# A conditioned transformer block on one core: query features scaled within FFN1, attention products at parts seven and ten of FFN2

## The chip, the cores and the metric

The kernel runs on one core of a Trainium2 chip. The metric is the device time of one execution in microseconds (us). Engines are named as in the profile: PE is TensorE (PEld its weight loads), DVE is VectorE, ACT is ScalarE, POOL is GpSimd, SP is SyncE, which here only issues DMAs. All times in the text are microseconds from the start of the profiled span unless said otherwise.

## The reference

A layer of 2048 rows of 576 with adaptive layer norm: linear attention with a softmax feature map in 32 heads of 18, then a dense ReLU network of width 4608. Cut to what matters:

```python
def _A_ref(x, wqkv, w_phi, wo):                  # per head, Dh = 18
    q, k, v = split(x @ wqkv)
    pq, pk = q @ w_phi, k @ w_phi
    phi_q = concat([softmax(pq), softmax(-pq)])
    phi_k = concat([softmax(pk), softmax(-pk)])
    kv, z = phi_k.T @ v, sum(phi_k, over rows)
    o = (phi_q @ kv) / (phi_q @ z + 1e-6)
    return o @ wo

sa, ca, ga, sb, cb, gb = split(silu(c) @ w_mod, 6)
x = x + ga * _A_ref(layernorm(x) * (1 + ca) + sa, ...)
h = layernorm(x) * (1 + cb) + sb
x = x + gb * (maximum(h @ w1, 0) @ w2)
```

## The kernel before

Rows are kept 128 to a tile, 16 tiles; a block is U = 2 tiles, so there are NQ = 8 blocks, 0 to 7. Everything up to the sum over keys (`kv`), and all of block 0's second half of the layer, runs in an order written out by hand, a string of steps. After it `block(n)` runs for n = 1 to 7, and the change lies in that function alone. Each engine executes its instructions in the order in which the code issues them, and waits where an operand or a buffer isn't ready; nothing is reordered.

`block(n)` does the dense network of block n, and between its matmuls two other jobs. The next block m = n + 1 gets its attention finished: output projection (`wo_rows`), residual, second layer norm, transposed into hT. The block after, n + 2, gets its query features made and its attention products taken.

**FFN1** (`ffn1_rows`, matmuls on line 827, ReLU on line 872). Nine pairs q of hidden tiles. Each is computed in two phases, "a" and "b", which use the two halves of the array's rows crosswise; the order on PE is a0, a1, b0, a2, b1, a3, b2 and so on to a8, b7, b8. Between a pair's phases stands a tiny POOL write, the token of line 831: phase b waits for it, and it waits for phase a. After b of pair q, ACT does the ReLU of q into H1. The products of a pair lie in one of three PSUM buffers (`mm_tile`), so phase a of pair q + 3 needs the ReLU of q. The dictionary `behind` says which other work is issued behind which phase: ("b", 5) is behind phase b of pair 5 and its ReLU.

**FFN2** (`ffn2_step`, line 910). For each of the two row tiles j and the two column halves (0 and 288) three parts of 12 matmuls, twelve parts in all. Part 0 takes one of the same three PSUM buffers, first that of FFN1's pair 6. Parts 0, 1 and 2 of each read the ReLUs of pairs 0 to 2, 3 to 5 and 6 to 8. After part 2 DVE scales the output (line 918), adds the residual (919), and after the second half SP sends it out (921).

**The features of block n + 2** (`softmax_parts`, in two tiles' E): `low` and `high` subtract the minimum and maximum (DVE, lines 464 to 479), `exps(j)` the exponential of tile j (ACT, 506), `sums(j)` their sums (DVE, 524), `recip` the reciprocal by Ln and Exp (ACT, 529 and 531), `scale` the scaling (DVE, 541, two instructions). `q_T` issues two DMA transposes on SP's queue (653), one for each tile, into ET. In traces E carries the name room.

**The attention products** `attention(m, j)`: `num` is 11 small matmuls (666) into the two aux PSUM buffers; `quotient` divides on DVE (674 to 681); `o_T` is a DMA transpose on SP (689). The aux buffers are also those of `wo_rows`.

**The next block's norm**: `late(j)` is the second phase of `wo_rows` (matmuls of line 827 too), the residual add on DVE (728) and the statistics on DVE (226, 227). `norm_out` is `rstd` on ACT (233, 234), the normalisation on DVE (238, two instructions), a copy (423), and two DMA transposes on SP into hT (425). `mods` scales hT in place on DVE (418, five instructions).

Before the change, the features of n + 2 are made in FFN1 up to the sums of tile 0. The sums of tile 1 come behind `norm_out` after FFN1; `recip`, `scale` and `q_T` come after FFN2's first three parts, behind their output on DVE. The products of tile 0 follow FFN2's seventh part, those of tile 1 the tenth. Block 1 differs in that it also takes the products of block 2, in FFN1. Block 6 has no features to make, block 7 no other work at all.

Of the kernel before, what the change touches and what calls it, by code (L numbers as in the profile page):

```python
# [21 lines left out]
NQ = NT // U  # L22
# [21 lines left out]
def kernel(  # L44
# [34 lines left out]
    def mm_tile(name):  # L79
        return mmp.tile([P, 2, 512], FP32, name=name, tag="mm")  # L80

    def aux_tile(name, dt=FP32):
        t = aux.tile([P, 512], FP32, name=name, tag="aux")
        return t if dt == FP32 else t.bitcast(BF16)
# [365 lines left out]
    HALVES = [(0, 288), (288, 288)]  # L450
# [148 lines left out]
    def q_soft(n):  # L599
        E = Eqs[n % 2]  # L600
        if n < 2:
            G.memset(E[:, :, :, DW:], 0.0)
        Es[n] = E
        b, u = n // 2, n % 2
        return softmax_parts(E[:, :, :, 0:DW], pq[b][:, u * U:(u + 1) * U], U, False)
# [42 lines left out]
    def q_T(n):  # L648
        E = Es[n]
        ET = work.tile([P, NG, U, P], BF16, name="ET", tag="ET", bufs=2)  # L650
        ETs[n] = ET
        for j in range(U):
            nc.sync.dma_start_transpose(out=ET[:, :, j, :], in_=E[:, j].rearrange("p g c -> p (g c)"))

    def num(n, j):

        ET = ETs[n]
        if n == 0:
            ps = mm_tile("ps_num")
            ps = (ps[:, 0], ps[:, 1])  # L660
        else:
            ps = (aux_tile("ps_num"), aux_tile("ps_nun"))
        onum[n, j] = ps
        for g in range(NG):
            o = (g % GB) * GV
            T_.matmul(ps[g // GB][:, o:o + gcols(g)], lhsT=ET[0:DW, g, j, :], rhs=KVZ[0:DW, g, 0:gcols(g)],  # L666
                      start=True, stop=True)
# [156 lines left out]
    def row_halves(key, phase, items):  # L824

        for k, (ps, l, r) in enumerate(items):
            i = T_.matmul(ps, lhsT=l, rhs=r, start=(phase == 0 and k < 2), stop=(phase == 1 and k >= len(items) - 2))  # L827
            if phase == 1 and k == 0:
                tc.add_manual_dep(i.ins, last[key].ins.name, AFTER, reason="same banks, other rows")
        if phase == 0:  # L830
            g = last[key] = G.memset(token[:], 0.0)  # L831
            tc.add_manual_dep(g.ins, i.ins.name, AFTER, reason="products of one half of the rows done")

    def f1_rows(n, q, phase):

        hT, w, items = hT2[n], U * P, []
        if phase == 0:
            f1_open(n, (q,))
        for hh in range(2):
            for ci in ((4, 0, 1, 2, 3) if phase == 0 else (0, 1, 2, 3)):  # L840
                for r in range(2):
                    s, e = slice(r * 64, r * 64 + 64), r ^ phase
                    l = w1["c"][s, 2 * q + hh, :] if ci == 4 else w1_at(2 * q + hh, e, ci, s)
                    items.append((f1[q][:, e, hh * w:hh * w + w], l, hT[s, ci, :]))
        row_halves(("f1", q), phase, items)

    def wo_rows(n, j, phase):

        if phase == 0:
            onum["wo", n, j] = [aux_tile("ps_wo") for _ in HALVES]  # L850
        items = []
        for ci in ((4, 0, 1, 2, 3) if phase == 0 else (0, 1, 2, 3)):
            for r in range(2):
                s, e = slice(r * 64, r * 64 + 64), r ^ phase
                items.append((onum["wo", n, j][e][:, 0:288], oTs[n, j][s, ci, :], wo_sb[s, ci, e * 288:e * 288 + 288]))
        row_halves(("wo", j), phase, items)

    def ffn1_rows(n, behind={}):

        for k in range(NI // 2 + 1):  # L860
            for p in (0, 1):
                q = k - p
                if k == 0 and p == 1 or q > NI // 2 - 1:
                    continue
                f1_rows(n, q, p)
                if p:
                    f1_relu(q)
                if ("ab"[p], q) in behind:
                    behind["ab"[p], q]()

    def f1_relu(q):
        A_.activation(out=p2t["H1"].rearrange("p (e j) n -> p e j n", e=2)[:, :, 2 * q:2 * q + 2],  # L872
                      in_=f1[q][:].rearrange("p e (h n) -> p e h n", h=2), func=ACT.Relu)
# [27 lines left out]
    def ffn2_step(n, j, cs, cn, part):  # L901

        if part == 0:
            f2[j, cs] = mm_tile("ps_y")
            if ("o", n, j) not in f2:
                f2["o", n, j], f2["sent"] = p2t["p2"].tile([P, D], BF16, name="outt", tag="outt", bufs=2), 0
        ps, o = f2[j, cs], f2["o", n, j]
        c = slice(cs, cs + cn)
        for k in [e * NI + part * 6 + i for e in range(2) for i in range(6)]:
            T_.matmul(ps[:, 0, 0:cn], lhsT=p2t["H1"][:, k, j * P:(j + 1) * P], rhs=p2t["w2"][:, k, c],  # L910
                      start=(k == 0), stop=(k == NJ - 1))
        if part == 2 and n > 0:
            ffn2_out(n, j, cs, cn)

    def ffn2_out(n, j, cs, cn):
        ps, o = f2[j, cs], f2["o", n, j]
        c = slice(cs, cs + cn)
        V.tensor_tensor(out=o[:, c], in0=ps[:, 0, 0:cn], in1=rows["gb"][:, c], op=ALU.mult)  # L918
        V.tensor_tensor(out=o[:, c], in0=o[:, c], in1=x_sb[:, n * U + j, c], op=ALU.add)
        if cs + cn == D or (n, j) == (NQ - 1, U - 1):  # L920
            nc.sync.dma_start(outv[:, n * U + j, f2["sent"]:cs + cn], o[:, f2["sent"]:cs + cn])
            f2["sent"] = cs + cn if cs + cn < D else 0

    def y(n, j, cols=HALVES):
        for cs, cn in cols:
            for part in range(3):
                ffn2_step(n, j, cs, cn, part)
# [74 lines left out]
    def block(n):  # L1002


        m = n + 1 if n + 1 < NQ else None
        if m is None:
            ffn1_rows(n)
            y(n, 0)

            y(n, 1, ((0, 288), (288, 192), (480, 96)))  # L1010
            return
        soft_ = q_soft(n + 2) if n + 2 < NQ else None
        xn, stats, rstd, norm = norm_stats(m * U, U)

        def do(name, *a):
            if soft_ is not None:
                getattr(soft_, name)(*a)

        def attention(m, j):
            num(m, j)  # L1020
            quotient(m, j)
            o_T(m, j)

        def late(j):
            wo_rows(m, j, 1)
            wo_out(m, j)
            stats(j)

        def norm_out():
            rstd()  # L1030
            norm()
            norm_dma(xn, U, new_hT2(m), 0)

        def mods():
            for ci in range(KC):
                modulate(V, hT2[m][:, ci, :], hT2[m][:, ci, :], mod[2], ci)

        def both(*fs):
            return lambda: [f() for f in fs]

        if n == 1:
            do("low")
            do("high")
            ffn1_rows(n, {("b", 0): lambda: attention(m, 0), ("b", 2): lambda: attention(m, 1), ("b", 3): lambda: do("exps", 0),
                          ("b", 4): both(lambda: wo_rows(m, 0, 0), lambda: do("exps", 1)), ("b", 5): both(lambda: late(0), lambda: do("sums", 0)),
                          ("a", 8): lambda: wo_rows(m, 1, 0), ("b", 7): lambda: late(1)})
        else:
            ffn1_rows(n, {("a", 0): both(lambda: do("low"), lambda: do("high")), ("b", 1): lambda: wo_rows(m, 0, 0),
                          ("b", 2): lambda: late(0), ("b", 3): lambda: do("exps", 0), ("b", 4): both(lambda: wo_rows(m, 1, 0), lambda: do("exps", 1)),
                          ("b", 5): both(lambda: late(1), lambda: do("sums", 0))})  # L1050
        norm_out()
        do("sums", 1)
        y(n, 0, HALVES[:1])
        do("recip", 0)
        do("scale", 0)
        if n + 2 < NQ:
            q_T(n + 2)
        ffn2_step(n, 0, 288, 288, 0)
        mods()
        ffn2_step(n, 0, 288, 288, 1)  # L1060
        ffn2_step(n, 0, 288, 288, 2)
        ffn2_step(n, 1, 0, 288, 0)
        if n + 2 < NQ:
            attention(n + 2, 0)
        ffn2_step(n, 1, 0, 288, 1)
        ffn2_step(n, 1, 0, 288, 2)
        ffn2_step(n, 1, 288, 288, 0)
        if n + 2 < NQ:
            attention(n + 2, 1)
        ffn2_step(n, 1, 288, 288, 1)  # L1070
        ffn2_step(n, 1, 288, 288, 2)

    for n in range(1, NQ):
        block(n)
# [28 lines left out]
```

## Time and profile before

| | |
|---|---|
| three runs, us | 414.24, 414.99, 414.65; median 414.65 |
| the profiled execution's own time, us | 414.88 |
| its span, us | 413.1 |
| DVE busy | 234.5 us, 57% |
| ACT busy | 178.6 us, 43% |
| DMA ET in the chain that ended last | 5% of the span |

The span runs from the first instruction of the program to the last; the execution's own time has 1.8 us more around it. A row of the timeline is start, length, engine, line, operation, output<-inputs with their shapes, and the number of instructions that it merges; in brackets stands the idle time ahead of it and what ended that. A row of waits is engine, line, what it waited for, then the total, the number of waits and the longest. Starts of PE's matmuls are good to follow; their lengths overlap, since matmuls are pipelined. Line numbers are those of the kernel before.

### The profile page before, as it was taken

The page shows a single profiled execution, that of the slowest core. Times are in us where ns is not written, and L with a number is a line of the kernel's source. Part 1 is how long each engine was busy: PE and PEld are TensorE (multiplying, and loading weights), DVE is VectorE, ACT ScalarE, POOL GpSimd, SP SyncE. Part 2 cuts the span into 40 slices and gives each one's busy share as a digit, 9 for nine tenths or more (in the row PEclk, how much of TensorE's full clock was granted, in tenths as well). Part 3 has the DMA queues.
Part 4 walks back from the last instruction along what each step waited for, and adds up shares of the span by engine and source line. Part 5 has one row for each costly group of instructions (what it writes and reads, how often), then busy time and mean ns, then how long its engine had stood idle before and what let it go on. Part 6 is the DMA issues. An engine that isn't in the chain of part 4 may idle for free.

```text
span 413.1 us, 11585 instructions
## 1 busy us (share of the span) xinstructions
PE 402.8 (98%) x5064; PEld 329.8 (80%) x5064; DVE 234.5 (57%) x600; ACT 178.6 (43%) x303; POOL 17.8 (4%) x112
## 2 busy tenths in 40 slices
PE   6999999999999999899999999999999999999997
PEld 3777777787887888688878887887788788878876
DVE  6889999989838556563566355536553731230011
ACT  5799999945751064006401530262046004402500
POOL 7100000000000000000000000000000000000000
PEclk9999999999999999999999999999999999999999
DMA  8967950499670630720061014105400520010000
GB/s 263 268 111 206 197 126 17 88 279 369 222 173 18 130 37 2 117 48 2 17 116 35 3 33 100 33 2 65 86 17 4 116 48 3 17 30 17 2 2 29
DMA packets 70988, 35.58 MB, mean 86 GB/s; under 512 B 56657, under 2 KB 67418, under 8 KB 70938
## 3 DMA queue, kind: packets, MB, share of 16 engines
q1 hardware_dynamic: 70336, 34.83, 36.2%
q8 instruction: 39, 0.64, 0.7%
q10 hardware_dynamic: 602, 0.02, 0.1%
q14 instruction: 11, 0.09, 0.1%
HBM read 19.27 MB, written 2.37 MB: 52 GB/s over the span
## 4 chain that ended last, share of the span: by engine, by line
PE 87%; DMA 8%; DVE 3%; issue 0%; SPq 0%; ACT 0%
PE ps_h L827 30%; PE ps_y L910 27%; DMA ET<-room 5%; PE ps_v L447 5%; PE ps_k L447 5%; PE ps_q L447 4%; PE ps_h L818 4%; PE ps_wo L827 3%; PE ps_sum L513 2%; DMA wma<-in_w_mod_dram 2%; DVE room L541 2%; PE ps_kv L625 1%; DMA kv_raw<-in_A_wqkv_dram 1%; PE ps_wo L447 1%; PE ps_num L666 1%; DVE outt L918 1%
## 5 line engine op out<-in xcount | busy, mean ns | idle before, releaser
L872 ACT ACTIVATE H<-ps_h 128x1024 bf16<-128x1024 f32 x72 | 72.7, 1022 | 172.2 <-PE ps_h L827 168.7
L910 PE MATMUL ps_y<-w_sb,H 128*128 128x288 bf16 (+2 forms) x1188 | 144.7, 282 | 0.0
L910 PEld LDWEIGHTS <-H 128*128 128x128 bf16 x1188 | 112.3, 98 | 28.1 <-issue 1.5
L827 PE MATMUL ps_h<-hT,w1a 64*128 64x256 bf16 x1120 | 70.9, 269 | 0.0
L827 PEld LDWEIGHTS <-w1a 64*128 64x128 bf16 x1120 | 54.5, 94 | 6.7
L827 PE MATMUL ps_h<-hT,w1b 64*128 64x256 bf16 x896 | 56.4, 269 | 0.0
L447 PEld LDWEIGHTS <-hT 128*128 128x128 bf16 x480 | 45.9, 97 | 12.6 <-issue 0.5
L918 DVE TENSOR_TENSOR outt<-ps_y,row_gb 128x288 bf16<-128x288 f32 (+2 forms) x33 | 14.8, 448 | 62.0 <-PE ps_y L910 61.9
L827 PEld LDWEIGHTS <-w1b 64*128 64x128 bf16 x896 | 43.6, 94 | 5.5
L728 DVE TENSOR_TENSOR x_sb<-x_sb,ps_wo 128x288 bf16<-128x288 bf16 x28 | 11.6, 451 | 53.3 <-PE ps_wo L827 52.0
L827 PE MATMUL ps_h<-hT,w1c 64*128 64x256 bf16 x252 | 34.4, 270 | 0.0
L238 DVE TENSOR_SCALAR xn<-x_sb,mv,rstd 128x576 bf16<-128x576 bf16 x32 | 12.3, 426 | 19.5 <-ACT rstd L234 19.4
L447 PE MATMUL ps_v<-wv_sb,hT 128*128 128x288 bf16 x160 | 21.6, 286 | 0.0
L447 PE MATMUL ps_q<-wfold,hT 128*128 128x270 bf16 (+1 forms) x160 | 21.4, 285 | 0.0
L447 PE MATMUL ps_k<-wfold,hT 128*128 128x270 bf16 (+1 forms) x160 | 21.4, 285 | 0.0
L831 POOL MEMSET token<- 1x2 bf16 x75 | 6.7, 89 | 336.4 <-PE ps_h L827 320.6
L506 ACT ACTIVATE room<-room 128x1188 bf16<-128x1188 bf16 x16 | 19.0, 1191 | 1.5 <-DVE room L479 1.5
L226 DVE BATCH_NORM_STATS2 bst<-x_sb 128x6 f32<-128x288 bf16 x46 | 18.5, 445 | 1.1 <-DMA x_sb<-in_A_x_dram 1.1
L524 DVE TENSOR_REDUCE ln_s<-room 128x66 f32<-128x1188 bf16 x14 | 19.0, 1366 | 0.0
L506 ACT ACTIVATE phik<-phik 128x2376 bf16<-128x2376 bf16 x8 | 17.4, 2186 | 0.0
L827 PE MATMUL ps_wo<-wo_sb,oT 64*128 64x288 bf16 x216 | 17.2, 283 | 0.0
L466 DVE TENSOR_TENSOR tree<-tree 128x264 bf16<-128x264 bf16 (+2 forms) x48 | 14.6, 305 | 1.7
(154 smaller groups left out, 400.5 us busy)
## 6 DMA issues: line engine op xcount, KB each, us to landing
w_sb<-in_B_w_dram SPq DMA_DIRECT2D x6, 864.0 KB, 7.5
out_dram<-outt SPq DMA_DIRECT2D x15, 144.0 KB, 1.8
w1b<-in_B_w_dram SPq DMA_DIRECT2D x2, 1024.0 KB, 9.6
x_sb<-in_A_x_dram SPq DMA_DIRECT2D x3, 576.0 KB, 7.3
w1a<-in_B_w_dram SPq DMA_DIRECT2D x2, 768.0 KB, 4.7
kv_raw<-in_A_wqkv_dram SPq DMA_DIRECT2D x4, 288.0 KB, 5.0
wma<-in_w_mod_dram SPq DMA_DIRECT2D x1, 1152.0 KB
wmb<-in_w_mod_dram SPq DMA_DIRECT2D x2, 576.0 KB, 4.1
```

The source lines that it names most:

```text
L226: V.bn_stats(out=st[:, half, :], in_=x_sb[:, t0 + j, half * 288:(half + 1) * 288])
L238: V.tensor_scalar(out=xn[:, j, 0:D], in0=x_sb[:, t0 + j, :], scalar1=mv[:, j, 0:1], scalar2=rs[:, j:j + 1], op0=ALU.subtract if by[j] == " ...
L447: T_.matmul(ps[:, 0:cn], lhsT=lhs[:, ci, :], rhs=w[:, ci, cs:cs + cn], start=(ci == 0), stop=(ci == KC - 1))
L466: V.tensor_tensor(out=a[:, :, 0:w], in0=a[:, :, 0:w], in1=a[:, :, w:2 * w], op=op)
L506: A_.activation(out=E[:, j:j + k], in_=E[:, j:j + k], func=ACT.Exp)
L524: V.tensor_reduce(out=t["l", b][:, k * 22:(k + 1) * 22].rearrange("p (g s) h -> p g s h", s=2), op=ALU.add, axis=mybir.AxisListType.X, in_ ...
L728: V.tensor_tensor(out=xs[:, cs:cs + cn], in0=xs[:, cs:cs + cn], in1=p[:, 0:cn], op=ALU.add)
L818: T_.matmul(f1[q][:, e, hh * w:hh * w + w], lhsT=w1_at(2 * q + hh, e, ci), rhs=hT[:, ci, :], start=(first and hh == 0 and ci == 0), stop=( ...
L827: i = T_.matmul(ps, lhsT=l, rhs=r, start=(phase == 0 and k < 2), stop=(phase == 1 and k >= len(items) - 2))
L872: A_.activation(out=p2t["H1"].rearrange("p (e j) n -> p e j n", e=2)[:, :, 2 * q:2 * q + 2], in_=f1[q][:].rearrange("p e (h n) -> p e h n" ...
L910: T_.matmul(ps[:, 0, 0:cn], lhsT=p2t["H1"][:, k, j * P:(j + 1) * P], rhs=p2t["w2"][:, k, c], start=(k == 0), stop=(k == NJ - 1))
L918: V.tensor_tensor(out=o[:, c], in0=ps[:, 0, 0:cn], in1=rows["gb"][:, c], op=ALU.mult)
```

## The change

In blocks 2 to 6 the steps move as follows. `exps` of tile 0 and 1 go behind pairs 2 and 3 (from 3 and 4); `sums` of tile 0 behind pair 4 (from 5); `sums` of tile 1 and `norm_out` behind pair 5 (from after FFN1), `recip` behind pair 6 and `scale` with `q_T` behind pair 7 (from after FFN2's third part). In block 1 `exps` and `sums` go as far forward, `recip` behind pair 5, `scale` and `q_T` behind pair 7, around `late(1)`; `norm_out` stays behind FFN1. In all of them the products of n + 2 are issued before the seventh and the tenth part of FFN2, where they stood after them; `mods` stays ahead of the fifth part. FFN2 is written as one loop. The number of instructions is the same on every engine.

```diff
+        def turn():
+            if n + 2 < NQ:
+                q_T(n + 2)
+
         if n == 1:
             do("low")
             do("high")
-            ffn1_rows(n, {("b", 0): lambda: attention(m, 0), ("b", 2): lambda: attention(m, 1), ("b", 3): lambda: do("exps", 0),
-                          ("b", 4): both(lambda: wo_rows(m, 0, 0), lambda: do("exps", 1)), ("b", 5): both(lambda: late(0), lambda: do("sums", 0)),
-                          ("a", 8): lambda: wo_rows(m, 1, 0), ("b", 7): lambda: late(1)})
+            ffn1_rows(n, {("b", 0): lambda: attention(m, 0), ("b", 2): both(lambda: attention(m, 1), lambda: do("exps", 0)),
+                          ("b", 3): lambda: do("exps", 1), ("b", 4): both(lambda: wo_rows(m, 0, 0), lambda: do("sums", 0)),
+                          ("b", 5): both(lambda: late(0), lambda: do("sums", 1), lambda: do("recip", 0)), ("a", 8): lambda: wo_rows(m, 1, 0),
+                          ("b", 7): both(lambda: do("scale", 0), lambda: late(1), turn)})
+            norm_out()
         else:
             ffn1_rows(n, {("a", 0): both(lambda: do("low"), lambda: do("high")), ("b", 1): lambda: wo_rows(m, 0, 0),
-                          ("b", 2): lambda: late(0), ("b", 3): lambda: do("exps", 0), ("b", 4): both(lambda: wo_rows(m, 1, 0), lambda: do("exps", 1)),
-                          ("b", 5): both(lambda: late(1), lambda: do("sums", 0))})
-        norm_out()
-        do("sums", 1)
-        y(n, 0, HALVES[:1])
-        do("recip", 0)
-        do("scale", 0)
-        if n + 2 < NQ:
-            q_T(n + 2)
-        ffn2_step(n, 0, 288, 288, 0)
-        mods()
-        ffn2_step(n, 0, 288, 288, 1)
-        ffn2_step(n, 0, 288, 288, 2)
-        ffn2_step(n, 1, 0, 288, 0)
-        if n + 2 < NQ:
-            attention(n + 2, 0)
-        ffn2_step(n, 1, 0, 288, 1)
-        ffn2_step(n, 1, 0, 288, 2)
-        ffn2_step(n, 1, 288, 288, 0)
-        if n + 2 < NQ:
-            attention(n + 2, 1)
-        ffn2_step(n, 1, 288, 288, 1)
-        ffn2_step(n, 1, 288, 288, 2)
+                          ("b", 2): both(lambda: late(0), lambda: do("exps", 0)), ("b", 3): lambda: do("exps", 1),
+                          ("b", 4): both(lambda: wo_rows(m, 1, 0), lambda: do("sums", 0)),
+                          ("b", 5): both(lambda: late(1), lambda: do("sums", 1), norm_out), ("b", 6): lambda: do("recip", 0),
+                          ("b", 7): both(lambda: do("scale", 0), turn)})
+        for j, cs, part in ((0, 0, 0), (0, 0, 1), (0, 0, 2), (0, 288, 0), (0, 288, 1), (0, 288, 2),
+                            (1, 0, 0), (1, 0, 1), (1, 0, 2), (1, 288, 0), (1, 288, 1), (1, 288, 2)):
+            if (j, cs, part) == (0, 288, 1):
+                mods()
+            if (j, cs, part) in ((1, 0, 0), (1, 288, 0)) and n + 2 < NQ:
+                attention(n + 2, cs // 288)
+            ffn2_step(n, j, cs, 288, part)
```

## The prediction

> **What bounds the kernel now.** I read the page first, then the matrix engine's waits, then the length of each block's second half, then the chain of waits through one of them, then the engines' timelines there.
>
> ```profile
> PE 402.8 (98%) x5064; PEld 329.8 (80%) x5064; DVE 234.5 (57%) x600; ACT 178.6 (43%) x303; POOL 17.8 (4%) x112
> PE ps_num L666 <- DMA ET<-room: 2.1, 2, 1.7
> PEld L666 <- DMA ET<-room: 3.9, 5, 2.0
> ```
>
> TensorE (PE) works nearly all the time, and no edit here takes a matmul away. What can be won is its waits only. The waits that recur name one transfer: ET, the transposed query features that the attention products (line 666) take as weights. Matmul and weight-load rows overlap, so I don't add them; I measure what they cost from the length of FFN2, the second half of a block. The windows below are FFN2 of blocks 1 to 6, cut at the first matmul of FFN2 and the first of the next FFN1 (the window, its length, busy time by engine, and at the end granted clock, 1.00 in all, DMA share and GB/s). The last row is FFN1 of block 5.
>
> ```profile
> 161.67:181.94 20.27, 18.54 (x168) 14.54 (x170) 11.37 (x32) 2.19 (x5) 0.00 (x0) 1.00 0.42 68
> 201.94:220.90 18.96, 18.55 (x169) 14.55 (x170) 10.44 (x29) 2.23 (x6) 0.00 (x0) 1.00 0.39 73
> 240.90:259.51 18.61, 18.55 (x168) 14.55 (x170) 10.44 (x29) 2.22 (x6) 0.00 (x0) 1.00 0.37 74
> 279.50:298.12 18.62, 18.55 (x169) 14.55 (x170) 10.53 (x29) 2.23 (x6) 0.00 (x0) 1.00 0.47 75
> 318.12:336.74 18.62, 18.55 (x168) 14.56 (x170) 10.44 (x29) 2.23 (x6) 0.00 (x0) 1.00 0.37 75
> 356.73:374.48 17.75, 17.75 (x147) 14.01 (x148) 4.64 (x14) 1.50 (x4) 0.00 (x0) 1.00 0.13 29
> 298.12:318.12 20.00, 20.00 (x362) 17.44 (x362) 9.81 (x25) 10.05 (x10) 0.98 (x11) 1.00 0.07 18
> ```
>
> Block 6 has no attention products and no wait: 17.75 us for twelve parts, 1.48 each. The other five have two sets of products. The second set of block 5 waits for nothing:
>
> ```profile
> 333.32 0.40 PE L666 MATMUL ps_num<-KVZ,ET 108*128 108x57 bf16 x8
> 333.64 1.63 PE L910 MATMUL ps_y<-w_sb,H 128*128 128x288 bf16 x12
> ```
>
> From its start to the next FFN2 matmul is 0.32, so an FFN2 without stalls should take 17.75 + 2 x 0.32 = 18.39. The excess is 1.88 in block 1, 0.57 in block 2, and 0.22, 0.23, 0.23 in blocks 3 to 5: 3.13 us together. The chain of waits says what makes it, here in block 5 (start, length, what):
>
> ```profile
> 318.12 4.53 PE ps_y L910 x36
> 322.67 0.47 DVE outt L918
> 323.47 1.39 DVE room L541 x2
> 324.91 3.62 DMA ET<-room
> 328.58 0.41 PE ps_num L666 x8
> ```
>
> Three parts of FFN2, VectorE's scaling of the first output half, only then the scaling of the features (line 541), their transposes, and at once the products. So the end is set by the scaling's place in VectorE's order, not by VectorE being busy (10.44 of 18.62). The same way takes 5.28 in the transfer of block 1, hence its larger stall.
>
> **The change, part by part.** Nothing is added or removed; all is order. In blocks 2 to 5, exponentials go one slot earlier, sums, normalisation, reciprocal, scaling and transposes into FFN1, and the products to the 7th and 10th part's start, one part (1.48) earlier than now. The need for ET in block 5 becomes 318.12 + 6 x 1.48 = 327.0. Now when is ET there? Today's rows of the engines concerned:
>
> ```profile
> 305.87 1.02 ACT L872 ACTIVATE H<-ps_h 128x1024 bf16<-128x1024 f32 x1 [1.55 <-PE ps_h L827]
> 309.25 1.19 ACT L506 ACTIVATE room<-room 128x1188 bf16<-128x1188 bf16 x1
> 312.87 1.02 ACT L872 ACTIVATE H<-ps_h 128x1024 bf16<-128x1024 f32 x1 [0.44 <-PE ps_h L827]
> 315.32 1.02 ACT L872 ACTIVATE H<-ps_h 128x1024 bf16<-128x1024 f32 x1 [1.43 <-PE ps_h L827]
> 317.29 1.94 ACT L872 ACTIVATE H<-ps_h 128x1024 bf16<-128x1024 f32 x2 [0.94 <-PE ps_h L827]
> 319.11 0.30 ACT L233 ACTIVATE rstd<-mv,eps_t 128x2 f32<-128x2 f32 x1
> 319.44 0.20 ACT L234 ACTIVATE rstd<-rstd 128x2 f32<-128x2 f32 x1
> 322.01 0.31 ACT L529 ACTIVATE ln_s<-ln_s 128x132 f32<-128x132 f32 x1 [2.37 <-DVE ln_s L524]
> 322.35 0.42 ACT L531 ACTIVATE rsum<-ln_s 128x264 bf16<-128x264 f32 x1
> 313.36 0.82 DVE L728 TENSOR_TENSOR x_sb<-x_sb,ps_wo 128x288 bf16<-128x288 bf16 x2 [5.21 <-PE ps_wo L827]
> 314.94 0.21 DVE L227 BATCH_NORM_AGGREGATE mv<-bst 128x2 f32<-128x12 f32 x1
> 315.07 1.34 DVE L524 TENSOR_REDUCE ln_s<-room 128x66 f32<-128x1188 bf16 x1
> 319.68 0.77 DVE L238 TENSOR_SCALAR xn<-x_sb,mv,rstd 128x576 bf16<-128x576 bf16 x2 [3.27 <-ACT rstd L234]
> 320.48 0.20 DVE L423 COPY xn<-xn 128x128 bf16<-128x128 bf16 x1
> 320.74 2.52 SPq L425 DMA_TRANSPOSE hT<-xn  x2
> 330.56 0.18 DVE L681 COPY o_tm<-o_tm 128x64 bf16<-128x64 bf16 x1
> ```
>
> *Exponentials.* They follow the ReLUs of pairs 2 and 3: 306.9 to 308.1, done before ReLU 3 (308.33), then 309.3 to 310.4, as today's first. No matmul waits. The first sum then fits VectorE's pause before line 728 of late(1) at 313.36, and stands no longer behind the statistics.
>
> *Wait on ScalarE.* The change puts rstd behind ReLU 5 (ends 313.9), where it waits for VectorE's statistics at 315.15; ReLUs 6 to 8 queue behind it. rstd takes 0.50, to about 315.7. ReLU 6, ready at 315.32, runs 315.7 to 316.7. The reciprocal (0.73 in two instructions) follows, its sums done at 315.1 + 1.4 = 316.5: 316.7 to 317.5. ReLU 7 ends at 318.5, ReLU 8 at 319.5. Who waits: FFN2's first matmul takes ReLU 6's PSUM buffer at 318.12, 1.4 later; part 3 reads ReLU 8's result at 318.12 + 2 x 1.48 = 321.1, 1.6 later. So the delays of 0.4 and 0.2 cost nothing, hidden by the matmuls of pairs 7 and 8. With that cover gone it would be 0.4 per block, some 2 us in five.
>
> *VectorE.* After the sum, normalisation 316.5 to 317.2, copy to 317.4, then the features' scaling (1.39 in the chain): 317.5 to 319.0. The outputs of FFN2 start at 322.67, so nothing of FFN2 waits for it. The scaling by mod, whose place on the matmul side stays, finds its hT earlier.
>
> *The sync queue (SP).* The two hT transposes issue at 317.6 and hold the queue 2.52, to 320.1; the two ET transposes, ready at 319.0, start then, and the output copy of this block still comes behind them. For the landing (counted from issue):
>
> ```profile
> DMA to landing us min/median/max: 3.5/3.7/5.3
> ```
>
> None of these rows has ET right behind hT, so I bound it: 3.5 if they don't disturb each other, 5.3 as the slowest seen plus the 2.52 of the hT pair if they serialise, 7.8. ET is there between 323.6 and 327.9; I take 3.7, the median, 323.8, since today's ET transposes too are issued one behind the other. Against 327.0, the middle has 3.2 us to spare and even 5.3 has 1.6; only the far end would cost 0.9 per block.
>
> *What is late next.* The first products at 327.0 need the two aux PSUM buffers, whose last reader is line 728 at 313.36 + 0.82. The second set, at 327.0 + 0.32 + 3 x 1.48 = 331.8, needs them back from the quotient, which ends today (line 681, 330.74) 2.2 after the products' start at 328.58. Now the output of part 6 comes first on VectorE (0.8 in the chain, 322.67 to 323.47): 327.0 + 0.8 + 2.2 = 330.0. It holds. The second set's own 0.32 stays.
>
> *Block 1* has its own order: reciprocal behind ReLU 5, scaling and transposes at slot b7.
>
> ```profile
> 157.77 1.02 ACT L872 ACTIVATE H<-ps_h 128x1024 bf16<-128x1024 f32 x1 [1.43 <-PE ps_h L827]
> 157.51 1.34 DVE L524 TENSOR_REDUCE ln_s<-room 128x66 f32<-128x1188 bf16 x1
> ```
>
> The second sum takes the place of the first, 157.5 to 158.9; reciprocal to 159.7; ReLU 6, ready at 157.77, ends at 160.7, and FFN2 needs its buffer at 161.67: 1.0 to spare, the tightest margin of the change. Scaling 159.7 to 161.1, ET issued at 161.1, landed by 166.4 at 5.3, needed at 161.67 + 8.9 = 170.5. Block 6 has no features to make; only rstd moves, into the same cover.
>
> **Sum.** 3.13 us of stalls go, nothing comes. The profiled execution took 414.88 (span 413.1): 414.88 - 3.13 = 411.75. The median, 414.65, is 0.23 lower, which gives 411.5. I say 411.6.
>
> One term speaks against it. POOL writes a token between the two phases of a pair; phase 1 waits for it.
>
> ```profile
> 316.50 0.09 POOL L831 MEMSET token<- 1x2 bf16 x1 [1.88 <-PE ps_h L827]
> 315.77 2.35 PE L827 MATMUL ps_h<-hT,w1b 64*128 64x256 bf16 x40
> 18.35 0.32 DVE L358 TENSOR_SCALAR wfold<-room,mod 128x576 bf16<-128x576 bf16 x1
> 18.39 0.11 POOL L557 MEMSET phik<- 128x20 bf16 x1
> ```
>
> The last token of block 5 falls at 316.50, where the moved normalisation and copy (316.5 to 317.4) now run. Pair 8's last 16 of these 40 matmuls begin about 318.05 - 16 x 0.057 = 317.1. If POOL were shut out until the copy ends, the token would be there at 317.5 and cost up to 0.4. The last two rows are the nearest case: a POOL memset that started 0.04 into a VectorE TENSOR_SCALAR took its ordinary 0.11. [...]
>
> **The rivals.**
>
> *Only blocks 1 and 2 gain (411.6 + 1.2 = 412.8).* Perhaps the first set of products costs 0.55 in itself, not 0.32, and blocks 3 to 5 hold no stall. Then 1.65 + 0.34 = 1.99 goes, beside 3.13. For it: matmuls of blocks 3 to 5 show under 0.1 idle. Against: their chain runs through ET with 0.04 between landing and products.
>
> *The token waits for the normalisation.* 0.4 in blocks 2 to 5 (block 6, with no sums, normalises 0.8 earlier): 411.6 + 1.6 = 413.2.
>
> *ScalarE becomes the gate, slower.* If the statistics reached VectorE behind both sums, rstd would be released at about 315.15 + 1.3 + 1.4 = 317.9, ReLU 6 end at 319.4, and TensorE stand 1.3 at FFN2's start in blocks 2 to 5: 411.6 + 5.2 = 416.8. It decides from 1.4 late on, and from 2.2 late (4 x 0.8 = 3.1) the change is a loss. For it: today the first sum does run behind the statistics. Against: it is now issued a slot before them, with its exponential done 5 us earlier.
>
> *ET does not come earlier.* If the sync queue held ET to its issue of today (324.9), the products, wanted one part sooner, would wait 1.48 more in five blocks: 414.65 + 7.4 = 422. For it: hT stands ahead in that queue. Against: hT leaves it at 320.1.
>
> **How the numbers follow.** Forecast 0.74, blocks 1 and 2 only 0.10, token 0.06, ScalarE 0.05, ET held 0.03, some other tie 0.02. 0.2%, about what a measurement of this kernel can tell, is 0.8 us, so faster means under 413.8: the first three, less 0.01 for a token that costs more, 0.89. Slower: the ScalarE and ET cases less a mild form of each, 0.07. Same: 0.04. The range: 411.0, where 0.6 more goes (run to run is 0.4 either way), to 413.0, which takes in the second case and most of the token's; it leaves out ScalarE, ET held, and some of the token: under 2 in 10.
>
> **What would show it.** Right: FFN2 of blocks 1 to 5 all near 18.4, no wait of line 666 for ET, ET issued near FFN2's start plus 2, FFN1 still 20.0. Wrong: FFN1 over 20.1, the first FFN2 matmul waiting for a ReLU, line 827 waiting for POOL, or ET landing after 8.9 us of FFN2.

## The result and the profile after

The changed kernel takes 411.68 us (median; 411.04 to 413.28) against 414.65 (414.01 to 415.43): a ratio of 0.9938, 95% interval 0.9915 to 0.9961. The prediction was 411.6, with a range of 411.0 to 413.0. Measured a second time, beside other runs of both, it took 411.18 against 414.70, ratio 0.9913 (0.9894 to 0.9931).

One thing has to be known to read the numbers: in part of the executions of either kernel TensorE's clock falls for a while in the start-up, which the mean granted clock shows as 0.996 instead of 1.000 and which costs 1.5 to 2 us. The profiled execution of the changed kernel, 413.17, is one of these; so the kernels are compared block by block below, behind the start-up.

The windows of FFN2 of blocks 1 to 6, cut as in the prediction, and of FFN1 of block 5, in the changed kernel:

```profile
163.14:181.52 18.38, 18.38 (x169) 14.64 (x170) 8.83 (x30) 1.52 (x3) 0.00 (x0) 1.00 0.42 84
201.52:219.90 18.38, 18.38 (x168) 14.63 (x170) 7.29 (x24) 1.10 (x2) 0.00 (x0) 1.00 0.42 84
239.90:258.27 18.37, 18.37 (x168) 14.62 (x170) 7.29 (x24) 1.10 (x2) 0.00 (x0) 1.00 0.41 84
278.27:296.65 18.38, 18.38 (x169) 14.64 (x170) 7.29 (x24) 1.11 (x2) 0.00 (x0) 1.00 0.63 83
316.65:335.03 18.38, 18.38 (x168) 14.64 (x170) 7.29 (x24) 1.10 (x2) 0.00 (x0) 1.00 0.47 85
355.02:372.77 17.75, 17.75 (x148) 14.01 (x148) 3.58 (x11) 1.11 (x2) 0.00 (x0) 1.00 0.18 28
296.65:316.65 20.00, 20.00 (x362) 17.46 (x362) 12.74 (x31) 11.06 (x14) 1.16 (x11) 1.00 0.04 12
```

Length and PE's busy time are now equal, so TensorE waits for nothing, and FFN1 has kept its 20.00 though DVE does 12.74 in it instead of 9.81. The five FFN2 are shorter by 1.89, 0.58, 0.24, 0.24 and 0.24: 3.19 us. The chain of work that ended last has no ET any more in blocks 1 to 5; of block 5 it reads:

```profile
316.65 8.93 PE ps_y L910 x72
325.88 4.42 PE ps_y L910 x36
330.61 4.42 PE ps_y L910 x36
335.03 5.13 PE ps_h L827 x92
```

What moved into FFN1 is seen in the timelines of ACT, DVE, SP and POOL around its end (FFN2 starts at 316.65):

```profile
311.40 1.02 ACT L872 ACTIVATE H<-ps_h 128x1024 bf16<-128x1024 f32 x1 [1.52 <-PE ps_h L827]
313.71 0.30 ACT L233 ACTIVATE rstd<-mv,eps_t 128x2 f32<-128x2 f32 x1 [1.29 <-DVE mv L227]
314.15 1.00 ACT L872 ACTIVATE H<-ps_h 128x1024 bf16<-128x1024 f32 x1
315.39 0.42 ACT L531 ACTIVATE rsum<-ln_s 128x264 bf16<-128x264 f32 x1
315.82 1.94 ACT L872 ACTIVATE H<-ps_h 128x1024 bf16<-128x1024 f32 x2
314.85 0.76 DVE L238 TENSOR_SCALAR xn<-x_sb,mv,rstd 128x576 bf16<-128x576 bf16 x2
315.85 1.47 DVE L541 TENSOR_TENSOR room<-room,rsum 128x1188 bf16<-128x1188 bf16 x2
315.90 2.53 SPq L425 DMA_TRANSPOSE hT<-xn  x2
318.54 3.69 SPq L653 DMA_TRANSPOSE ET<-room  x2
315.03 0.27 POOL L831 MEMSET token<- 1x2 bf16 x1 [1.88 <-PE ps_h L827]
```

rstd waits 1.29 on ACT with three ReLUs behind it; ReLU 6 runs 314.15 to 315.15 and leaves 1.5 us to FFN2's start. The scaling ends at 317.3, but ET is issued at 318.54, when hT leaves SP's queue, 1.9 us into FFN2. Over all ET transposes, both of each pair, the landing reads

```profile
DMA to landing us min/median/max: 3.6/3.8/5.3
```

The products wait for the first of a pair. In blocks 2 to 5 it lands 5.5, 5.5, 6.9 and 6.1 us into FFN2, and the products start 8.9 in.

### The profile page after: what moved, and what is told of

Read it like the earlier page. It is cut to its first block, busy times and chain, and to the rows that moved or that the text cites. A ratio compares the mean times of both kernels' runs of the same rounds, so it can differ in the third digit from the quotient of the medians.

```text
span 411.4 us, 11586 instructions
## 1 busy us (share of the span) xinstructions
PE 403.1 (98%) x5063; PEld 330.2 (80%) x5064; DVE 233.9 (57%) x600; ACT 178.2 (43%) x303; POOL 18.6 (5%) x112
## 4 chain that ended last, share of the span: by engine, by line
PE 95%; DMA 3%; DVE 0%; ACT 0%; SPq 0%; issue 0%
PE ps_y L910 35%; PE ps_h L827 30%; PE ps_v L447 5%; PE ps_k L447 5%; PE ps_q L447 4%; PE ps_h L818 4%; PE ps_wo L827 3%; PE ps_sum L513 2%; DMA wma<-in_w_mod_dram 2%; PE ps_kv L625 1%; PE ps_wo L447 1%; DMA kv_raw<-in_A_wqkv_dram 1%; PE ps_num L666 1%; PE ps_bias L366 1%; PE ps_h L810 1%; PE ps_fold L345 0%
## 5 line engine op out<-in xcount | busy, mean ns | idle before, releaser
L226 DVE BATCH_NORM_STATS2 bst<-x_sb 128x6 f32<-128x288 bf16 x46 | 18.6, 445 | 1.0 <-DMA x_sb<-in_A_x_dram 1.0
L827 PEld LDWEIGHTS <-w1c 64*128 64x128 bf16 x252 | 12.3, 94 | 3.4 <-issue 1.7
```

The source lines that it names most:

```text
L226: V.bn_stats(out=st[:, half, :], in_=x_sb[:, t0 + j, half * 288:(half + 1) * 288])
```

## The experiments

All kernels ran beside the kernel before on the same chips, and each ratio is against that. The changed kernel at full clock takes 411.1 us (median of ten runs).

**Products back behind parts seven and ten** (e1), all else as changed:

```diff
-            if (j, cs, part) in ((1, 0, 0), (1, 288, 0)) and n + 2 < NQ:
-                attention(n + 2, cs // 288)
             ffn2_step(n, j, cs, 288, part)
+            if (j, cs, part) in ((1, 0, 0), (1, 288, 0)) and n + 2 < NQ:
+                attention(n + 2, cs // 288)
```

> The changed kernel with the attention products put back behind the seventh and tenth part; the features stay early. Theory (the gain is that ET lands before the products want it): in the changed kernel ET is issued 1.9 us after FFN2's start and lands some 3.8 later, at 5.7, against a need at 8.9; at 10.3 it is just as early, so FFN2 stays 18.4 in blocks 1 to 5 and the whole is that of the changed kernel, 411.1 to 411.7, within 0.4. Rival (the place of the products at the border of two row tiles is worth something itself): FFN2 over 18.5, the whole 0.5 to 1 us slower than the changed kernel.

Measured: 412.11, ratio 0.9917 (0.9891 to 0.9942); its three runs at full clock are 411.24, 411.48 and 411.50. Line 666 waits for ET nowhere, and FFN2 takes 18.4 in each of blocks 1 to 5, as in the changed kernel. The place of the products brings nothing of its own; what counts is that ET is there.

**The products alone moved** (e2), in the kernel before:

```diff
-        ffn2_step(n, 1, 0, 288, 0)
         if n + 2 < NQ:
             attention(n + 2, 0)
+        ffn2_step(n, 1, 0, 288, 0)
...
-        ffn2_step(n, 1, 288, 288, 0)
         if n + 2 < NQ:
             attention(n + 2, 1)
+        ffn2_step(n, 1, 288, 288, 0)
```

> The kernel before with nothing but the products one part earlier; features as before. Theory: ET's landing doesn't move, so every block 1 to 5 waits one part, 1.48 us, more: 5 x 1.48 = 7.4 over the kernel before, 422.0; waits of line 666 for ET about 1.5 to 3.3 each. Rival (products earlier help by themselves, or the wait is hidden): at or under the kernel before, 414.6.

Measured: 421.35, ratio 1.0145 (1.0117 to 1.0174). The wait that the change removes is back, and longer:

```profile
PE ps_num L666 <- DMA ET<-room: 8.2, 5, 2.1
```

The direction is the theory's, and so is the size in blocks 2 to 5, whose FFN2 is 1.45 to 1.67 longer. Block 1 gives nothing (20.1 for 20.27), which leaves the whole short of 7.4: its ET landed in 3.62 us in this run where it had taken 5.28 before; e8 below says why.

**Products still earlier** (e3), in the changed kernel ahead of parts four and seven:

```diff
-            if (j, cs, part) in ((1, 0, 0), (1, 288, 0)) and n + 2 < NQ:
-                attention(n + 2, cs // 288)
+            if (j, cs, part) in ((0, 288, 0), (1, 0, 0)) and n + 2 < NQ:
+                attention(n + 2, j)
```

> The changed kernel with the products still earlier, ahead of the fourth and the seventh part (4.44 and 8.9 us into FFN2). Theory: ET lands 5.7 us into FFN2 in blocks 2 to 5, so TensorE waits 5.7 - 4.4 = 1.3 in each, 5.2 us together; block 1 issues ET 0.4 before FFN2's start and lands 3.4 to 4.9 in, so 0 to 0.5 there: 5.2 to 5.7 over the changed kernel, 416.3 to 417.4. Rival (landing is no issue any more, margins are wider than the rows say): as the changed kernel.

Measured: 418.43, ratio 1.0067 (1.0038 to 1.0096); its runs at full clock are 416.71, 416.73 and 417.87. The waits:

```profile
PE ps_num L666 <- DMA ET<-room: 5.3, 4, 2.2
```

Four blocks wait 5.3 together and block 1 does not. That the sum meets the 5.2 worked out is in part luck: blocks 2 to 4 wait 1.0 to 1.1 each, and block 5 waits 2.2, as its ET took 4.75 to land with a fetch packet in its way (e8). So the margin of the change is known from both sides: products at 8.9 us into FFN2 wait for nothing, at 4.4 they wait 1.0 to 2.2.

**Only the scaling ahead of FFN2** (e4), in the kernel before:

```diff
-        y(n, 0, HALVES[:1])
         do("recip", 0)
         do("scale", 0)
         if n + 2 < NQ:
             q_T(n + 2)
+        y(n, 0, HALVES[:1])
```

> The kernel before with one thing moved: reciprocal, scaling and the ET transposes ahead of FFN2's first part, still after FFN1, so that the scaling is no longer behind the first output on VectorE. Theory: the reciprocal still waits for the second sum (ends 4 us into FFN2), so the scaling starts at 322.8 instead of 323.5 in block 5 and ET comes 0.7 earlier: blocks 2 to 5 lose their whole stall (0.57 + 0.68), block 1 0.7 of 1.88, 1.95 in all: 412.7. Rival (scaling isn't what ET waits for, or the output pushed back costs): 414.6 or more.

Measured: 412.87 (412.12 to 414.16), ratio 0.9941 (0.9919 to 0.9964). One wait is left, in block 1:

```profile
PE ps_num L666 <- DMA ET<-room: 1.2, 1, 1.2
```

FFN2 of blocks 2 to 5 is down to 18.4 or 18.5, that of block 1 to 19.7. ET is issued 0.6 us earlier, and these few lines alone bring 1.7 of the 3.2 us that the change takes from FFN2. This shows the prediction's reading of the chain: ET waited for the scaling's place behind FFN2's first output on DVE.

**The normalisation back behind FFN1** (e5), in the changed kernel, blocks 2 to 6:

```diff
-                          ("b", 5): both(lambda: late(1), lambda: do("sums", 1), norm_out), ("b", 6): lambda: do("recip", 0),
+                          ("b", 5): both(lambda: late(1), lambda: do("sums", 1)), ("b", 6): lambda: do("recip", 0),
                           ("b", 7): both(lambda: do("scale", 0), turn)})
+            norm_out()
```

> The changed kernel with the next block's normalisation put back behind FFN1 in blocks 2 to 6; only the features stay early. Theory (the gain is the features' alone): FFN2 stays 18.4 in blocks 1 to 5, the whole is that of the changed kernel within 0.4, 411.1 to 411.7; the tokens of POOL all take their 89 ns again, since no normalisation runs beside them. Rival (the early normalisation is part of the gain): 0.5 us or more slower than the changed kernel.

Measured: 411.51 (410.54 to 411.80), ratio 0.9902 (0.9880 to 0.9925), and the tokens, the three times being shortest, median and longest:

```profile
L831 POOL MEMSET token<- x75: 89/89/91, 141.6 to 387.2; 1x2 bf16 x75
```

So the early normalisation is no part of the gain, and it is what makes a token 0.27 long in the changed kernel.

**ScalarE held up ahead of ReLU 6** (e6). It adds three copies on ACT whose results nobody reads:

```diff
+        def idle():
+            for _ in range(3):
+                A_.activation(out=x_sb[:, 0, :], in_=x_sb[:, 1, :], func=ACT.Copy)
...
-                          ("b", 5): both(lambda: late(1), lambda: do("sums", 1), norm_out), ("b", 6): lambda: do("recip", 0),
+                          ("b", 5): both(lambda: late(1), lambda: do("sums", 1), norm_out, idle), ("b", 6): lambda: do("recip", 0),
```

> The changed kernel with three extra copies on ScalarE (576 wide, 0.68 each, into rows that nobody reads any more) behind rstd in blocks 2 to 6, ahead of ReLU 6: 2.05 us. Theory (ScalarE's wait is hidden as long as ReLU 6 ends before FFN2's first matmul): the margin in the changed kernel is 1.5 (ReLU 6 ends at 315.15, FFN2 starts at 316.65), so TensorE waits 2.05 - 1.5 = 0.55 at FFN2's start in five blocks, 2.7 us over the changed kernel. Rivals: no cover, every 0.1 on ScalarE costs 0.1 (5 x 2.05 = 10 us over it); or a cover so wide that nothing is lost.

Measured: 414.50, ratio 0.9990 (0.9972 to 1.0009). The wait is where it was expected, five times, and about as long (0.56 each):

```profile
PE ps_y L910 <- ACT H L872: 2.8, 5, 0.6
```

FFN1 of blocks 2 to 6 is 0.62 longer each, 3.1 together; the copies took 2.10, which is 0.6 over the margin. The first 1.5 us of delay are free, what comes beyond costs its full length in every block, and 2 us of work a block on an engine that is busy 43% of the time have eaten nearly the whole gain.

**VectorE busy beside the tokens** (e7). It adds work whose results nobody reads, in block 7:

```diff
         if m is None:
+            for _ in range(10):
+                V.tensor_scalar(out=x_sb[:, 0:4, :], in0=x_sb[:, 4:8, :], scalar1=eps_t[:], scalar2=eps_t[:], op0=ALU.mult, op1=ALU.add)
+            for _ in range(6):
+                V.tensor_tensor(out=x_sb[:, 0:4, :], in0=x_sb[:, 4:8, :], in1=x_sb[:, 8:12, :], op=ALU.add)
             ffn1_rows(n)
```

> The changed kernel with VectorE kept busy through FFN1 of block 7, in rows that nobody reads any more: ten TENSOR_SCALAR of 128x2304 bf16 (estimate 0.87 each from 0.343 at 256 and 0.426 at 576), then six TENSOR_TENSOR of 128x2304 (some 1.4 each). Theory (a one-input bf16 TENSOR_SCALAR shuts POOL out until it ends, as the token of 0.27 beside the normalisation suggests): the tokens of the first four or five pairs take up to 0.9 instead of 0.09 and the phases behind them start late by what exceeds 0.5, FFN1 of block 7 up to 1.5 longer than 17.8; the tokens beside TENSOR_TENSOR take 0.09. Rival (the 0.27 has another cause): all tokens 0.09, FFN1 17.8.

Measured once: 412.65. The tokens of the block, and what DVE does meanwhile:

```profile
373.50 0.34 POOL L831 MEMSET token<- 1x2 bf16 x1 [20.60 <-PE ps_h L827]
374.59 0.16 POOL L831 MEMSET token<- 1x2 bf16 x1 [0.76 <-PE ps_h L827]
376.56 0.09 POOL L831 MEMSET token<- 1x2 bf16 x1 [1.80 <-PE ps_h L827]
378.52 0.09 POOL L831 MEMSET token<- 1x2 bf16 x1 [1.88 <-PE ps_h L827]
380.49 0.68 POOL L831 MEMSET token<- 1x2 bf16 x1 [1.88 <-PE ps_h L827]
382.45 0.09 POOL L831 MEMSET token<- 1x2 bf16 x1 [1.28 <-PE ps_h L827]
372.93 9.12 DVE L1008 TENSOR_SCALAR x_sb<-x_sb,eps_t 128x2304 bf16<-128x2304 bf16 x10
382.08 8.32 DVE L1010 TENSOR_TENSOR x_sb<-x_sb 128x2304 bf16<-128x2304 bf16 x6
```

Three of the five tokens beside TENSOR_SCALAR are stretched, all beside TENSOR_TENSOR are ordinary. The instructions of the first kind follow each other every 0.91, at 373.84, 374.75 and so on, and the stretched tokens end there (373.50 + 0.34, 374.59 + 0.16): POOL waited until the running instruction ended, then got in between. These three began 0.23 to 0.75 into an instruction. Of the two ordinary ones, that at 376.56 fell between two instructions, but that at 378.52 began 0.10 into one (from 378.42) and was not held. FFN1 of the block stayed 17.79, against up to 1.5 more in the theory. My allowance of 0.5 was too small there: behind phase a of a pair come b of the pair before and a of the next, some 2 us, before its phase b; only the last pair has 0.6.

**The instruction fetch moved** (e8), in the kernel before. It adds 56 matmuls at the start whose results nobody reads:

```diff
+    def tiny(n):
+        ps = aux_tile("ps_warm")
+        for _ in range(n):
+            T_.matmul(ps[:, 0:8], lhsT=zeros[:, 0:P], rhs=zeros[:, 0:8], start=True, stop=True)
...
-    LP.1 LP.0 Z.20 LS.1 LS.0 LK.4 ...
+    LP.1 LP.0 Z.20 Y0.56 LS.1 LS.0 LK.4 ...
```

> The kernel before with 56 tiny matmuls (8 columns, result unused) added at its start, where TensorE waits for its first data; all later instructions of TensorE thus come 112 places later, and the instruction fetches (one packet of 16 KB each) fall elsewhere against the work. Theory (the 5.28 us of ET's transfer in block 1 of the kernel before, where the others take 3.6, is a fetch packet that falls within it and holds one DMA engine up): at 6.9 us a fetch in FFN1 and some 13 in FFN2, the fetch of block 1 moves from 3.4 us after ET's issue to about 2 before it; ET lands in 3.6 to 3.8 there, FFN2 of block 1 takes 18.6 instead of 20.27, unless another block is hit instead. Rival (block 1's transfer is long for a reason of its own, such as its neighbours in the queue): 5.0 to 5.3 again, FFN2 of block 1 20.3.

Measured once: 417.26, with a mean clock of 0.992, lost in the start-up, so that its time says nothing; block 1 does. First the DMAs of the kernel before between ET's issue and landing in block 1, then those of this kernel (queues with packets, MB and share; issues with the time to landing):

```profile
q1 hardware_dynamic: 2164, 0.55, 90.1%
q8 instruction: 1, 0.02, 1.0%
ET<-room SPq DMA_TRANSPOSE x2, 5.2
```

```profile
q1 hardware_dynamic: 2049, 0.52, 73.2%
ET<-room SPq DMA_TRANSPOSE x2, 3.7
```

```profile
166.11:184.71 18.60, 18.55 (x169) 14.56 (x170) 11.36 (x32) 2.19 (x5) 0.00 (x0) 1.00 0.37 75
```

The last row is FFN2 of block 1. The fetch (queue 8) came 4.7 us ahead of ET's issue here, not about 2. With no fetch packet in the window the transfer takes 3.7, and FFN2 of block 1 18.60 instead of 20.27, as blocks 3 to 5 of the kernel before. Block 2 too is at 18.6 here, instead of 18.96; the fetch packet in its ET's way is gone as well. So 2.0 of the 3.19 us that the change gains in FFN2 hung on where fetches fell in this one build. The other 1.2, about 0.24 a block, are the stall that is left when none falls there.

**Start-up filled** (e9, and again e11 beside the changed kernel, e10). It adds four 512-wide matmuls on zeros ahead of the first modulation products:

```diff
-    ... FA1.3 MC1.1 LP4.6 ...
+    ... FA1.3 Z.40 Z.41 Z.42 Z.43 MC1.1 LP4.6 ...
```

> The changed kernel with four 512-wide matmuls on zeros (result unused, 0.86 us at full clock) ahead of the first modulation products, in the start-up where TensorE waits for a weight. Theory (runs whose mean granted clock is 0.996 are those in which TensorE stood idle over half of 13 to 15 us, so that the clock fell to 0.66 in 15 to 20): with the gap filled no run shows 0.996, all lie at 411.0 to 412.2, which is 0 to 0.8 over the undisturbed runs of the changed kernel (411.1) for the added work. Rival (the clock falls for another reason): about one run in three is 2 us longer at 0.996 as before.

> The changed kernel again, beside the next one on the same chip, to count its runs at a mean granted clock of 0.996. Theory (a waiting TensorE in the start-up lets the clock fall): about one run in three or more at 0.996 and 413.2, the others 411.0 to 411.7. Rival (chance of the chip and hour): none.

> The changed kernel with four matmuls on zeros in the start-up, as in e9_fill, again. Theory: no run at 0.996, all 411.2 to 412.0, so that its median is at or under that of the changed kernel and its highest run over 1 us under. Rival: as many runs at 0.996 as the changed kernel, each at 413.5.

Measured: e9 411.40 (411.23 to 411.92), ratio 0.9889 (0.9867 to 0.9911); e11 411.57 (411.33 to 411.77), ratio 0.9923 (0.9908 to 0.9937). All ten runs are at full clock, while seven of the 18 runs of the kernel before beside them are at 0.995 or 0.996. But e10, without the filling, also had none in its six (411.18, 410.42 to 411.72), against my one in three. The filling costs about 0.4 where nothing falls; that it keeps the clock up, these runs don't show.

## Why the prediction was right

**What bounds the kernel.** Right: only waits could go, and all of those in FFN2 were ET's. e2 brings the wait back and e4 removes over half of it by the scaling's place alone.

**The sum.** 3.13 predicted, 3.19 measured over the five blocks. The 0.22 of blocks 3 to 5, the term that the second case doubted, was a stall: each of these blocks lost 0.24, and e1 loses it too with the products where they stood. The medians differ by 2.97, or by some 3.5 in the second measurement. What lies between 3.2 and 3.5 is outside the FFN2 of blocks 1 to 5 and not settled; FFN1 kept its length. That 411.6 lies so near the 411.68 measured is in part luck: three of those seven runs lost some 2 us to the clock in the start-up, and at full clock the kernel takes 411.1, 0.5 less than predicted.

**ScalarE's cover.** Margin 1.4 predicted for ReLU 6, 1.5 in the trace; in block 1, 1.0 predicted and 1.1 in the trace. The price beyond it, 1 for 1 in each block, is shown by e6.

**ET's landing.** 2.0 us into FFN2 for the issue and 5.7 for the landing predicted; 1.9 and 5.5 measured in blocks 2 and 3, and 6.9 and 6.1 in blocks 4 and 5, where a fetch packet fell in its way. The far end, 5.3 + 2.5, did not occur: blocks 2 and 3 land in 3.6 from the issue with hT right ahead, as blocks 3 to 5 did before without. e3 shows the 5.5 as a wait.

**Block 1.** Its excess was right as a sum, but the prediction took its 5.28 as that transfer's own; e8 shows a fetch packet behind it. The same holds for the 0.34 by which block 2 stood over blocks 3 to 5. The change takes these away not by moving the fetches but by its margin of 2.0 us and more, which covers them where they fall now.

**The token.** The case was a small one and stayed so: the last token is late by 0.19 (0.27 for 0.09), since POOL got in after the first of the two normalisation instructions and not after the copy, and 0.5 was there to spare. That POOL would be shut out was my assumption, which no row of the kernel before showed, and the 0.4 up to the copy's end no run shows. Here the nearest row that I chose, a memset of 0.11 that started 0.04 into a TENSOR_SCALAR, misled; e7 shows the blocking. In the changed kernel and in e7, tokens that began 0.18 to 0.75 us into a TENSOR_SCALAR (0.42 long in the one, 0.88 in the other) ended 0.03 to 0.07 after it, and did not wait for the engine to fall idle. e7's token at 0.10 and that memset at 0.04 were not held, and why these got in stays open. The case's own price, 413.2, also lay above the range's end of 413.0, so the range did not take in most of it.

**Slower cases.** Neither came. e6 shows the first gate, 1.5 us of delay beyond where this order stands; e2 shows the price of products that are wanted sooner than ET comes. For the latter this order has 2.0 to 3.4 us to spare.

## What to carry to other kernels

Where the bounding engine waits for a transfer, follow the chain back to the instruction whose place in its engine's order makes the transfer late: here a scaling stood behind an output that itself waited for matmuls, on an engine only half busy. Work may then be moved into the stretch before at no cost as long as each instruction queued behind the new wait has a measured margin: write that margin down, since in e6 delay was free up to it, 1.5 us, and paid one for one in every block beyond. And ask of the longest stall whether it is the same in other builds; a chance such as a fetch can be most of it, here 1.7 of 1.9 us.

## What was not expected of the hardware

**A fetch of instructions held up a data transfer.** One 16 KB packet (the kernel before has 39 of them, 0.64 MB), 1.0% of the time of the DMA engines in the window, went with 5.2 instead of 3.7 us for ET to land; e8 took the packet away and the time with it. It is so in all 13 profiles, over blocks 1 to 5: the first ET transpose of a block landed in 3.60 to 3.65 us in the 38 cases without a fetch packet in its time, and in 3.8 to 5.6 in the 19 in which one began in it. (In the other eight the packet began ahead of the issue; 3.6 to 4.8.) In FFN1 of block 5 of the kernel before, which holds two of them, TensorE itself lost nothing: it is busy 20.00 of 20.00 us. ET's landing did lose by this one.

**The clock in the start-up.** The windows of the changed kernel's profiled execution, then of the kernel before (PE's busy time first, granted clock third from the end):

```profile
13.00:15.00 2.00, 0.84 (x24) 0.58 (x22) 1.19 (x3) 0.81 (x2) 0.00 (x0) 1.00 0.98 331
15.00:20.00 5.00, 5.00 (x73) 3.04 (x70) 4.26 (x15) 2.91 (x6) 1.19 (x8) 0.66 1.20 269
```

```profile
13.00:15.00 2.00, 1.70 (x45) 1.57 (x43) 1.68 (x5) 1.17 (x4) 0.00 (x0) 1.00 0.99 340
15.00:20.00 5.00, 4.98 (x80) 3.75 (x78) 4.60 (x19) 4.26 (x10) 1.37 (x9) 1.00 1.45 238
```

Where TensorE waited for a weight and was busy 0.84 of 2 us, its clock fell to 0.66 of full in the next 5 us: from 16.18 to 19.59, for 3.41 us, it was at 0.50, ahead of that and behind it at 1.00. Where it was busy 1.70 it didn't fall. In the profiles of the kernel before, the changed kernel and e1 to e10 it fell at 0.44 (e8), 0.84 and 1.25 (e1) busy of these 2 us and not from 1.35 on. e8 shows 0.50 over 15 to 20. As little as 0.75 us of waiting within the 2 (e1) went ahead of a fall. None of the ten runs with the filling shows the fall, but the changed kernel beside it had none either, so it isn't shown that the filling prevents it.
